# Chunk 0 of six batches: the second expert product by plain matmuls in place of a seven-product block scheme

## The chip, the cores and the metric

The kernel runs on one core of a Trainium2 chip. The metric is the device time of one execution in microseconds. The kernel before was timed in three runs. The profiler also left one execution of it, with the start and end of nearly every instruction on TensorE (PE for matmuls, PEld for the loads of their stationary operand), VectorE (DVE), ScalarE (ACT), GpSimd (POOL) and the queues of the DMAs.

## What is computed

The input is `x` of 8 batches, 2496 rows and 256 columns. Each batch goes through a spectral step and then through one expert of a small mixture of experts.

```python
X = np.fft.rfft(x, axis=1)
Yr = Xr @ w_r - Xi @ w_i + b_r ;  Yi = Xr @ w_i + Xi @ w_r + b_i
Y = shrink(Yr) + 1j * shrink(Yi)        # sign(v) * max(|v| - 0.01, 0)
y = np.fft.irfft(Y, n=2496, axis=1)
e = argmax(softmax(mean(y) @ w_gate))   # one expert per batch
out[b] = gate * (relu(y[b] @ w1[e]) @ w2[e])
```

`w1[e]` is 256 x 1024 and `w2[e]` 1024 x 256. The change lies in the last product, `h @ w2[e]`, whose inner length is 1024.

## The kernel before

**The work of a batch.** The transform of 2496 = 39 x 64 points is done in two steps by matmuls with tables. For batches 2 to 7 (`add_attn`) a forward step over 39 points (line 869) is evicted to `A`, goes through DRAM to `XB`, and is followed by a step over 64 points (L933, evicted to `XT` at L941), the products with the mixed weights (L971), a bias and sum on VectorE (`tt` L985, `z` L995), the shrink (`cl` L1004, `Y` L1010), and the inverse step over 64 points with 64 rows of the array at a time (L599). After another way through DRAM the last inverse step (L1109) is evicted to `ysb` (L1125, L1131). Batches 0 and 1 go through `add_attn_direct` with other shapes.

**The expert's part** (`add_moe`) cuts the 2496 rows of batches 1 to 7 into chunks of 512 rows, c = 0 to 3, and a last one of 448. For each chunk the first product is eight groups of two matmuls of 512 columns (L1445), each evicted with a relu into the tile `hs` (L1458 on ScalarE or L1460 on VectorE). The second product has two forms, and the set `FAST` (L398) says which chunk gets which.

- **Plain form** (L1469 to L1558). A chunk has two tiles of 256 rows. Each tile is 16 matmuls of 256 columns (L1496), four groups of four, into one PSUM bank. One eviction of 128 x 512 then multiplies by the gate (L1513 on ScalarE, L1516 on VectorE), and one DMA stores 256 rows (L1536).
- **Block form** (`add_fast`, L1256). The product is split into 2 x 2 blocks by rows and by inner halves and columns, and done with seven block products in place of eight. VectorE makes four sums of `hs` halves (L1274, L1277, L1281, L1284; 128 x 1024 each). Seven block products of eight matmuls of 128 columns follow (L1307). Four results are taken from PSUM with the gate (L1322 on ScalarE, or L1325 on VectorE), three are added onto them on VectorE (L1331), and two DMAs store 256 rows each (L1358). The block form also needs four sums of `w2` blocks for each batch, `T` (L1249, `add_weight_sums`), which serve all chunks of that batch.

Before the change chunks 0 to 3 of batches 1 to 7 use the block form, 28 chunks. The last chunk of a batch has one plain tile and one turned tile (`add_turned`, L1378, L1393 to L1415); batch 7's last chunk has two plain tiles.

**The order of the work** is not written by hand. Every operation is given to a small planner (`Schedule`) with modelled costs, its dependencies, its buffers and a due time. The planner repeatedly emits the operation that can start first on its engine by its model, and of those that tie the one with the earlier due time. Evictions may go to ScalarE or VectorE, whichever the planner finds free. The order so found is static for each engine; a change of one operation's kind can so reorder others. In units of a period's 44th from a batch's start, the plain groups of chunk 0 are due at 6 to 13, the block products of chunk 0 at 8 to 15.2 with stores at 16, and the first products of chunk 1 at 8 to 15.

**Buffers around it.** `hs` has two buffers. PSUM has four banks "a", two "h" (first product) and two "o" (second product); in batches 1 to 6 a block-form chunk holds both "o" banks from its first products to its last additions, and a plain tile holds one. The sums of `hs` have one buffer, `S`, so the sums of a chunk wait for the last product that reads those of the chunk before. The output tiles `ost` have four buffers.

Of the kernel before, what the change touches and what calls it, by code (L numbers as in the profile page):

```python
# [17 lines left out]
B = 8  # L18
# [232 lines left out]
def kernel(  # L251
# [143 lines left out]
    W_LATE, B_LATE = 46.0, 53.5  # L395
    WARM, COLD, WARM_END = 60, 12, 11.9
    LATE = -0.12
    FAST = {(B - 1, c) for c in range(4)} | {(b, c) for b in range(1, B - 1) for c in (0,1,2,3,)}  # L398
    PERIOD, SPAN, SHIFT = 49.5, 1.4, 0.6

    ps = psum.tile([P, 8, 512], FP32, name="ps")
# [835 lines left out]
    def add_weight_sums(b, w, wk, v):  # L1237
        tk = S.tok("T", 1)

        t_ops = []  # L1240
        for i in (0, 1, 2, 3):
            def ts(_, i=i):
                if i == 0:
                    T_t[b] = spool.tile([P, 4, 4, P], FP16, name="T")
                T = T_t[b]
                w2 = w2s_t[b].rearrange("p (k i) (h c) -> p k h i c", k=2, h=2)
                x, y = ((w2[:, 0, 1], w2[:, 0, 0]), (w2[:, 1, 1], T[:, 0]),
                        (w2[:, 1, 1], w2[:, 0, 1]), (w2[:, 1, 0], T[:, 1]))[i]
                nc.vector.tensor_sub(out=T[:, i], in0=x, in1=y)  # L1249
            t = S.op("DVE", 0.35, ts, v, deps=[w] + t_ops[-1:], lat=0.48,  # L1250
                     allocs=[] if i else [tk])
            wk.rel.append(t)
            t_ops.append(t)
        return t_ops, tk
# [166 lines left out]
    def add_moe(b, y_ops, yk, gate):  # L1421
        w, gb_op, wk = gate
        v0 = b * PERIOD
        if any(x == b for x, _ in FAST):
            t_op = add_weight_sums(b, w, wk, v0 - 0.05 * PERIOD)
            t_first = t_op[0][0]
        for c, (ns, nl, tiles) in enumerate(NCH0 if b == 0 else NCH):
# [36 lines left out]
            if c == 0 and 0 < b < B - 1:  # L1464
                t_first.after = h_ops[0]
            if (b, c) in FAST:
                add_fast(b, c, ns, nl, cell, h_ops, hk, wk, t_op, gb_op, v0)
# [136 lines left out]
```

## Time and profile before

| | |
|---|---|
| three runs | 430.68, 429.89, 430.34 us; median 430.34 |
| the profiled execution | 430.68 us, its span 428.9 us |
| granted TensorE clock | 1.000 over the span |
| busy share of the span | PE 97%, PEld 73%, DVE 80%, ACT 83%, POOL 14% |
| DMA | 77.72 MB, mean 181 GB/s |

The span runs from the first to the last instruction. A PE row is drawn longer than the time that it keeps the array, since the next matmul starts before the one before it has drained: a matmul of 128 columns shows a mean of 219 ns. What a matmul costs a stream of matmuls is read from the chain of work that ended last, which gives runs of equal matmuls from start to start. Idle time of an engine that is not the bottleneck costs nothing.

### The profile page before, as it was taken

How to read it: one execution, taken by the hardware profiler on the slowest of the kernel's cores; microseconds unless marked ns; L12 is line 12 of the kernel's file. 1: busy time of each engine (PE TensorE's matmuls, PEld its weight loads, DVE VectorE, ACT ScalarE, POOL GpSimd, SP SyncE). 2: the span in 40 equal slices, each digit the busy share in tenths (PEclk: the TensorE clock that was granted, in tenths of full speed). 3: DMA queues.
4: the chain of work that ended last, by engine and by line, in shares of the span. 5: the costliest groups of instructions: out<-in, count | busy, mean ns of one | idle time of the engine just before them, and what ended most of it. 6: DMA issues, size and time to landing. Idle time of an engine off the chain costs nothing.

```text
span 428.9 us, 11121 instructions
## 1 busy us (share of the span) xinstructions
PE 415.3 (97%) x4297; PEld 311.9 (73%) x4297; DVE 344.6 (80%) x667; ACT 357.3 (83%) x742; POOL 60.7 (14%) x104
## 2 busy tenths in 40 slices
PE   5888999999999999999999999999999999999996
PEld 2557777887677867778677876778677876777775
DVE  1697875767889899898998889988998989966661
ACT  3788888888978798888978799787978888788884
POOL 5463100001003020033002120031200030001000
PEclk9999999999999999999999999999999999999999
DMA  8899797939786996879985997969976294532222
GB/s 148 228 172 166 129 274 241 252 92 178 205 265 126 226 219 200 265 131 232 198 235 176 217 214 196 287 109 240 210 210 227 76 198 93 166 108 79 66 100 92
DMA packets 70973, 77.72 MB, mean 181 GB/s; under 512 B 7144, under 2 KB 43712, under 8 KB 70920
## 3 DMA queue, kind: packets, MB, share of 16 engines
q1 hardware_dynamic: 57954, 56.88, 45.4%
q0 software_dynamic: 12704, 19.88, 29.2%
q8 instruction: 33, 0.54, 0.5%
q10 hardware_dynamic: 262, 0.25, 0.2%
q14 instruction: 20, 0.16, 0.1%
HBM read 58.20 MB, written 37.49 MB: 223 GB/s over the span
## 4 chain that ended last, share of the span: by engine, by line
PE 87%; DVE 7%; ACT 2%; DMA 2%; issue 1%; POOL 1%; DVEq 0%; POOLq 0%
PE ps L1445 30%; PE ps L1307 21%; PE ps L971 8%; PE ps L1496 7%; PE ps L599 4%; PE ps L1109 4%; PE ps L869 3%; PE ps L775 3%; PE ps L933 3%; PE ps L1378 2%; DMA xin<-in_x_dram 2%; DVE tt L985 1%; DVE z L823 1%; DVE z L995 1%; PE ps L811 1%
## 5 line engine op out<-in xcount | busy, mean ns | idle before, releaser
L1458 ACT ACTIVATE hs<-ps 128x512 f16<-128x512 f32 (+3 forms) x307 | 167.5, 575 | 31.2 <-PE ps L1445 27.0
L1445 PE MATMUL ps<-ysb,w1s 128*128 128x512 f16 (+3 forms) x688 | 179.6, 359 | 0.3 <-ACT hs L1458 0.3
L1445 PEld LDWEIGHTS <-w1s 128*128 128x128 f16 x688 | 68.0, 113 | 22.2 <-issue 2.4
L1307 PEld LDWEIGHTS <-hs 128*128 128x128 f16 x896 | 58.1, 98 | 17.9 <-issue 2.5
L1322 ACT ACTIVATE ost<-ps,gbc 128x256 f32<-128x256 f32 x111 | 53.8, 485 | 9.2 <-PE ps L1307 8.4
L1331 DVE SCALAR_TENSOR_TENSOR ost<-ps,gbc,ost 128x256 f32<-128x256 f32 x84 | 40.4, 480 | 18.9 <-ACT ost L1322 12.7
L1307 PEld LDWEIGHTS <-S 128*128 128x128 f16 x672 | 42.9, 98 | 11.3 <-issue 0.4
L971 PE MATMUL ps<-w,XT 128*128 128x256 f16 x360 | 49.9, 273 | 0.0
L971 PEld LDWEIGHTS <-XT 128*128 128x128 f16 x360 | 34.8, 98 | 12.8 <-DVE XT L952 0.2
L995 DVE TENSOR_TENSOR z<-ps,tt 128x512 f16<-128x512 f32 x60 | 39.3, 685 | 2.5 <-PE ps L971 1.3
L1496 PE MATMUL ps<-w2s,hs 128*128 128x256 f16 x288 | 40.7, 272 | 0.0
L985 DVE TENSOR_TENSOR tt<-ps,bias 128x1024 f16<-128x1024 f32 x30 | 36.6, 1221 | 4.2 <-PE ps L971 3.8
L1307 PE MATMUL ps<-T,hs 128*128 128x128 f16 x448 | 34.2, 219 | 0.0
L1307 PE MATMUL ps<-w2s,hs 128*128 128x128 f16 x448 | 34.2, 219 | 0.0
L1125 ACT CAST ysb<-ps 128x468 f16<-128x468 f32 (+1 forms) x67 | 31.7, 526 | 2.8 <-PE ps L1109 1.9
L879 ACT CAST A<-ps 120x512 f16<-120x512 f32 x57 | 32.9, 622 | 0.8 <-PE ps L869 0.3
L1307 PE MATMUL ps<-T,S 128*128 128x128 f16 x448 | 32.7, 219 | 0.0
L941 ACT CAST XT<-ps 128x512 f16<-128x512 f32 x52 | 30.1, 613 | 0.2 <-PE ps L933 0.2
L1496 PEld LDWEIGHTS <-hs 128*128 128x128 f16 x288 | 26.9, 98 | 3.9
L1460 DVE TENSOR_SCALAR hs<-ps 128x512 f16<-128x512 f32 (+3 forms) x37 | 21.2, 588 | 10.3 <-PE ps L1445 9.9
L609 ACT CAST V<-ps 128x512 f16<-128x512 f32 x42 | 23.7, 601 | 5.5 <-PE ps L599 5.4
L1201 POOL DMA_DIRECT2D w1s<-in_moe_w_dram x8 | 6.0, 754 | 123.9 <-DVE z L995 67.3
(116 smaller groups left out, 631.5 us busy)
## 6 DMA issues: line engine op xcount, KB each, us to landing
out_dram<-ost SPq DMA_DIRECT2D x71, 256.0 KB
scr<-V SPq DMA_DIRECT2D x35, 256.0 KB
xin<-in_x_dram POOLq DMA_DIRECT2D x21, 390.0 KB, 9.0
XB<-fwd SPq DMA_DIRECT2D x30, 256.0 KB
V<-scr SPq DMA_DIRECT2D x14, 504.0 KB
fwd<-A SPq DMA_DIRECT2D x18, 360.0 KB
w1s<-in_moe_w_dram POOLq DMA_DIRECT2D x8, 512.0 KB, 6.3
w2s<-in_moe_w_dram POOLq DMA_DIRECT2D x8, 512.0 KB, 7.9
```

The costliest lines, as they stand in the source:

```text
L879: COPY[eng](out=A_t[b][:, 2 * gp : 2 * gp + 2, :].rearrange("p g c -> p (g c)"), in_=cell["p"][0:120, :])
L941: COPY[eng](out=cell["X"][:, ch, :, 0:2].rearrange("p a r i k -> p a i r k"), in_=hc["p"].rearrange("p (a i r k) -> p a i r k", a=2, i=2, ...
L971: nc.tensor.matmul(pm[:, D * a : D * a + D], cell["X"][:, ch, a, t].rearrange("p i k -> p (i k)"), w4[:, ch, t, :], start=(ch == 0), stop= ...
L985: nc.vector.tensor_add(out=cell["tt"], in0=cell["T", 2].rearrange("p (a c) -> p a c", a=2).unsqueeze(1).to_broadcast([P, 2, 2, D]), in1=bi ...
L995: nc.vector.tensor_add(out=cell["z"][:, r], in0=cell["T", 1 - r].rearrange("p (a c) -> p a c", a=2), in1=cell["tt"][:, r])
L1125: COPY[eng](out=yv[:, :, 12 * gb : 12 * gb + 3 * nf].rearrange("p a (g j) -> p a g j", j=3), in_=pi[:, 0 : 117 * nf].rearrange("p (g a j) ...
L1307: nc.tensor.matmul(fc[dst[0]][0:m, dst[1], t, :], A[a](f, t), bb(f), start=start and t == 0 and f == 0, stop=f == 3, skip_group_check=True)
L1322: nc.scalar.activation(out=ost(t, h), in_=src, func=AFT.Copy, scale=gbc_t[b][0:m])
L1331: nc.vector.scalar_tensor_tensor(out=ost(t, h), in0=fc["F"][0:m, half], scalar=gbc_t[b][0:m], in1=ost(t, h), op0=ALU.mult, op1=ALU.add)
L1445: nc.tensor.matmul(ph[:, 0:nl], w1v[:, ch, fc // 4, :, fc % 4], ysb_t[b][:, ch, ns : ns + nl], start=(ch == 0), stop=(ch == 1))
L1458: nc.scalar.activation(out=o, in_=i, func=AFT.Relu)
L1496: nc.tensor.matmul(oc["p"][:, i, :], cell["hs"][:, ft, ts], w2s_t[b][:, ft, :], start=(ft == 0), stop=(ft == E - 1))
```

## The change

Chunk 0 of batches 1 to 6 leaves the set `FAST`. These six chunks are computed in the plain form; chunks 1 to 3 of those batches and chunks 0 to 3 of batch 7 stay in the block form. Nothing else is edited.

```diff
-    FAST = {(B - 1, c) for c in range(4)} | {(b, c) for b in range(1, B - 1) for c in (0,1,2,3,)}
+    FAST = {(B - 1, c) for c in range(4)} | {(b, c) for b in range(1, B - 1) for c in (1,2,3,)}
```

The set is read in two places: at L1424, where the sums `T` are made for each batch that has any chunk in it (batches 1 to 7 still do), and at L1466, where a chunk takes the one form or the other. A short label that came with the change speaks of an inverse step in half-array matmul pairs and a shrink in one operation over all partitions. The diff touches neither; the inverse step at L599 and the shrink at L1004 and L1010 stay as they are.

## Prediction

> **What bounds the kernel now.** I read the page first: busy shares, then the costliest groups.
>
> ```profile
> span 428.9 us, 11121 instructions
> PE 415.3 (97%) x4297; PEld 311.9 (73%) x4297; DVE 344.6 (80%) x667; ACT 357.3 (83%) x742; POOL 60.7 (14%) x104
> L1322 ACT ACTIVATE ost<-ps,gbc 128x256 f32<-128x256 f32 x111 | 53.8, 485 | 9.2 <-PE ps L1307 8.4
> L1331 DVE SCALAR_TENSOR_TENSOR ost<-ps,gbc,ost 128x256 f32<-128x256 f32 x84 | 40.4, 480 | 18.9 <-ACT ost L1322 12.7
> ```
>
> PE is busy for 97% of the span. A PE row is modelled, though, so the share alone doesn't say that PE is the limit. Next come the windows: four equal stretches of 49.5 us, a batch each, and the two that follow.
>
> ```profile
> 139.50:189.00 49.50, 49.46 (x539) 37.35 (x536) 44.91 (x86) 43.15 (x94) 7.59 (x13) 1.00 0.86 207
> 189.00:238.50 49.50, 49.46 (x539) 37.34 (x537) 44.91 (x86) 43.14 (x94) 7.70 (x13) 1.00 0.87 208
> ...
> 337.50:387.00 49.50, 48.73 (x540) 36.84 (x538) 41.28 (x76) 40.65 (x88) 3.71 (x6) 1.00 0.51 125
> 387.00:428.90 41.90, 38.01 (x405) 28.94 (x401) 21.42 (x41) 31.09 (x67) 2.28 (x4) 1.00 0.25 86
> ```
>
> After the start and length stand PE, PEld, DVE, ACT, POOL, the clock (1.00), the DMA share and GB/s. In a full period PE is without work for 0.04 us, DVE for 4.6, ACT for 6.4. From 90 to 337.5 us the list of waits names no wait of a matmul at all (only of weight loads, 0.4 us at most). In 337.5 to 387 it names two (0.44 us for `tt` L985, 0.29 us for `hs` L1458), and PE is idle for 0.77 us.
>
> The third view is the chain of work that ended last. In a full period every piece of it is PE. These pieces (start, length, what, how many) give the prices:
>
> ```profile
> 170.32 0.87 PE ps L971 x8
> ...
> 175.59 0.54 PE ps L599 x8
> 176.14 1.00 PE ps L1307 x16
> ...
> 179.77 0.89 PE ps L1307 x16
> ...
> 342.80 0.88 PE ps L1496 x8
> ```
>
> Sixteen matmuls of 128 columns take 0.89 us, so 55.6 ns each. Eight of 256 columns take 0.87 (L971) or 0.88 us (L1496), so 109 to 110 ns. Behind a group of L599, which uses half the rows, the next group is some 0.11 us longer (1.00 against 0.89), whichever it is.
>
> Is anything hidden in "busy"? I add up a period at these prices. L1445: 64 x 216.5 ns + 16 x 190 = 16.9 us (pairs of 0.43 and 0.38); L1307: 224 x 55.6 = 12.45; L971: 60 x 109 = 6.54; L599: 40 x 67.5 = 2.70; L1109: 42 x 52 and two short ones = 2.23; L869: 11 x 216 = 2.38; L933: 40 x 56 = 2.24; L1496: 16 x 109 = 1.74; L1378: 16 x 82.5 = 1.32; the gate 0.1. That is 48.6 us, and five L599 groups with 0.11 behind each make it 49.15. The period is 49.5, so 0.35 us is left open. **PE's own work is the bound, and the others' slack is real.** A microsecond taken from DVE is worth nothing here; a microsecond added to PE costs a microsecond.
>
> **The change, part by part** (six chunks, one in each of batches 1 to 6).
>
> PE: each chunk loses seven block products, 56 matmuls of 128 columns: 56 x 55.6 ns = 3.11 us. It gains 32 matmuls of 256 columns: 32 x 109.5 = 3.50 us. That is +0.39 us a chunk, at most +0.41 (0.88 us for eight). A lower price: L1307 holds 25.8% of the chain of a full period, 12.77 us or 3.19 a chunk, because some L599 pauses stand before it; against 3.49 the difference is 0.30. Those pauses don't leave with the form, so I take 0.385. **Six chunks: +2.3 us**, bounds 1.8 and 2.45.
>
> A rule that speaks against this: the Trainium skill, "TensorE: Matmul & The Clock Gate", section "Back-to-back issue gap", says that in a stream of weight loads and matmuls the loads count too, and gives about 81 ns for a matmul of 128 columns and about 131 ns for 512. By it, and with about 98 ns for 256 columns drawn between the two, an estimate from that page, a chunk would go from 4.5 to 3.1 us and the change would win some 8 us. The 0.89 us for sixteen in this trace, each with a load of its own, speaks for 55.6 ns, and the trace decides.
>
> DVE: each chunk loses four sums of 0.683 us (L1274 to L1284) and three additions of 0.480, together 4.17 us. ACT: it loses four takes of 0.485 us (1.94) and gains two evictions of 128x512 at 0.689 us (L1513; 0.751 if VectorE takes one), so -0.56 us. In a period DVE goes from 44.9 to about 40.7 us. Both lie beside PE's 49.5, so I count them at **nothing**. What could be regained is bounded by PE's idle time: 0.04 us a period, 0.15 in 90 to 139.5, 0.77 in 337.5 to 387. In that last stretch the 0.29 and 0.44 us end at 350.87 and 357.35; the first sum of batch 6's chunk 0 (L1274) begins at 357.21. Most of that idle time comes before the sums that go, and the sums `T` (four of 0.42 us, 350.7 to 353.5) stay, as chunk 1 needs them. I take 0, with -0.9 as the end of all idle time regained.
>
> Buffers, waits and queues, all with one answer. A plain tile holds one "o" bank where the block form held both. The sums of chunk 1 no longer wait for chunk 0's use of `S`. `hs` is held until the last plain group, as it was until the last block product. An eviction now waits for sixteen matmuls; behind it on ACT stand relu evictions with 6.4 us of slack a period. Two stores of 256 KB go to SP's queue before and after, due a little earlier. The weight load and its GpSimd DMAs don't move. Cost: nothing, and if that cover fails, PE shows it as a wait.
>
> The order: the planner finds a new one, and no row shows it. Where PE is packed, a different order of the same work costs nothing. Where DVE holds the chain, at 101 to 110 us and 352 to 357 us, an unlucky order could make PE wait for a `tt` (1.22 us) once more, and a lucky one saves the idle time above. I take 0, which is nearest to the windows' idle times, with +1.2 and -0.9 as ends.
>
> **Sum.** The profiled execution took 430.68 us (span 428.9 and 1.78 around it), the slowest of the three; +2.3 gives 433.0. Against the median 430.34 that is 432.6, which I forecast. The own range of this case: 430.34 + 1.8 - 0.9 = 431.2 to 430.34 + 2.45 + 1.2 = 434.0.
>
> **Rivals.**
>
> *Faster, as VectorE is relieved.* Mechanism: the 0.9 us by which a period (49.5) exceeds my sum of PE's work (48.6) is not the pause behind L599 but PE waiting for evictions inside rows drawn as busy; with 4.2 us less on DVE these waits go. All of it: six chunks x (0.385 - 0.9) = -3.1, less 0.77 in the stretch after 337.5 us = -3.9, so 426.5; with half of the 0.9 it is 429.2. It decides from 0.385 us regained a batch. For it: DVE is above 90% busy in the periods, and the matmul ends are modelled. Against it: no DVE or ACT piece in the chain of a period, no wait of PE in the list, and the 0.11 us stands behind L599 at regular places.
>
> *Slower by more, through the order.* In both stretches where DVE holds the chain the new list puts the second product ahead of the eviction that PE needs next, and PE waits for a `tt` and two `z` (1.22 + 1.28 us) in each: 2 x 2.5 + 2.3 = +7.3, so up to 437.6; half of that is 435.3. For it: the work is placed statically by modelled costs. Against it: evictions have more slack than before.
>
> *No difference.* The diff doesn't do what its label says (inverse and shrink stay), and if the plain groups fill pauses that the block products can't, the extra 0.385 us is absorbed: 430.3. Against it: there is no PE idle time to fill in a period.
>
> **How the numbers follow.** Forecast 0.70, faster through VectorE 0.10, slower through the order 0.14, no difference 0.06. A measurement of this kernel can tell about 0.2%, or 0.86 us, from no change: the bounds are 429.5 and 431.2. Faster takes 0.08 of the first rival. Same takes its other 0.02, the 0.06 of no difference, and 0.02 of the forecast's low end: 0.10. Slower is 0.82. The range goes from 430.2, which takes in no difference, to 434.6, which takes in the forecast and nearly half of the slower rival: about 0.82 in all.
>
> **What would show it.** PE should lose 336 rows of L1307 and gain 192 of L1496, whose runs of eight in the chain still take 0.87 to 0.88 us. DVE's busy time should fall by about 25 us (6 x 4.17) to some 320 and ACT's by about 3. The windows of a period should be 49.9 us long with PE idle for less than 0.1, and the last instruction of batch 1's stretch should be late by 0.4, batch 6's by 2.3. If the span grows by more, the list of waits should name PE waiting for DVE or ACT around 100 to 110 or 345 to 365 us. The prediction is wrong in its core if a period becomes shorter than 49.5 us, for then PE's busy rows held waits.

## The result and the profile after

The changed kernel takes 435.35 us (median of four runs, 434.92 to 435.77) against 430.51 for the kernel before. The ratio is 1.0114, with a 95% interval of 1.0097 to 1.0132. The forecast was 432.6 in a range that ended at 434.6: the sign was right, and the loss was about twice as large. The profiled executions have spans of 428.9 and 434.0 us, so 5.1 us are to be found.

From the page of the kernel after, the busy shares and the two groups that show the change:

```profile
span 434.0 us, 10803 instructions
PE 418.2 (96%) x4153; PEld 312.3 (72%) x4153; DVE 330.6 (76%) x635; ACT 353.2 (81%) x720; POOL 60.6 (14%) x104
L1496 PE MATMUL ps<-w2s,hs 128*128 128x256 f16 x480 | 69.3, 273 | 0.0
L1331 DVE SCALAR_TENSOR_TENSOR ost<-ps,gbc,ost 128x256 f32<-128x256 f32 x66 | 31.6, 479 | 14.1 <-ACT ost L1322 10.3
```

L1496 has 192 more matmuls, L1331 18 fewer additions, and VectorE is busy for 14 us less in all (not the 25 of the sum, since the planner gave it more evictions: `V` L609 24 times in place of 18, `A` L879 14 in place of 9). The windows of the kernel after:

```profile
139.50:189.00 49.50, 48.79 (x498) 36.34 (x496) 41.65 (x75) 41.09 (x86) 7.59 (x13) 1.00 0.83 204
189.00:238.50 49.50, 48.79 (x493) 36.39 (x493) 41.61 (x78) 41.07 (x87) 6.11 (x11) 1.00 0.84 202
```

PE, first after the length, now idles for 0.71 us in each of these stretches, where it idled for 0.04. VectorE is less busy than before, and yet PE waits. The list of waits of PE names one line, in the full periods (us in total, times, the longest):

```profile
PE ps L599 <- DVE tt L985: 2.7, 4, 0.7
```

Where do the 5.1 us lie? A mark that each batch has once is the load of `w2` (L1206). It fetches the weights of the batch that comes next, so the stretch from one mark to the following one holds the chunks of one batch. Two of its starts in the kernel after:

```profile
150.84 0.73 POOL L1206 DMA_DIRECT2D w2s<-in_moe_w_dram  x1 [5.30 <-PE ps L1109]
201.68 0.71 POOL L1206 DMA_DIRECT2D w2s<-in_moe_w_dram  x1 [5.28 <-PE ps L1109]
```

From mark to mark a period is 50.84 us; it was 49.51. The table has all such stretches. The last column is for a kernel told below, the block form with a repaired planner:

| from mark to mark, us | before | after | difference | block form, repaired |
|---|---|---|---|---|
| batch 1 | 49.36 | 49.42 | +0.06 | 48.71 |
| batches 2 to 5, each | 49.50 | 50.85 | +1.34 | 49.50 |
| batch 6 to the end | 80.18 | 79.78 | -0.40 | 79.47 |

The four periods together make +5.37, and with 0.07 ahead of batch 1 and -0.34 in the other two rows the sum is 5.1. So the whole loss lies in the four packed periods, 1.34 us in each, of which the prediction's price of the plain form explains 0.385.

**What PE waits for.** The timeline of the kernel after, in the first full period (start, length, engine and line, what; some of PE's rows, and VectorE's `tt`):

```profile
156.04 0.60 PE L1496 MATMUL ps<-w2s,hs 128*128 128x256 f16 x4
...
156.48 0.38 PE L869 MATMUL ps<-xin,wa 117*120 117x512 f16 x1
...
157.57 0.60 PE L971 MATMUL ps<-w,XT 128*128 128x256 f16 x4
...
158.00 0.60 PE L869 MATMUL ps<-xin,wa 117*120 117x512 f16 x2
158.20 1.22 DVE L985 TENSOR_TENSOR tt<-ps,bias 128x1024 f16<-128x1024 f32 x1
...
158.53 0.28 PE L599 MATMUL ps<-Y,ti 64*128 64x256 f16 x1
159.48 0.59 PE L599 MATMUL ps<-Y,ti 64*128 64x256 f16 x7 [0.67 <-DVE tt L985]
```

And the same place in the kernel before:

```profile
155.93 0.81 PE L869 MATMUL ps<-xin,wa 117*120 117x512 f16 x3
...
157.44 0.60 PE L971 MATMUL ps<-w,XT 128*128 128x256 f16 x4
...
157.88 0.61 PE L1307 MATMUL ps<-w2s,hs 128*128 128x128 f16 x8
158.08 1.23 DVE L985 TENSOR_TENSOR tt<-ps,bias 128x1024 f16<-128x1024 f32 x1
158.42 0.61 PE L599 MATMUL ps<-Y,ti 64*128 64x256 f16 x8
```

In both, `tt` runs while PE comes to the third L599 group of a batch. Before, the group's eight matmuls run through. After, one runs, and the other seven wait until `tt` has ended. An L599 group writes two PSUM banks in turn, the first matmul to the one and the second to the other. The four "a" banks are handed out in a ring. Before, the ring ran L869 (three banks), L971, then L599's two: these were banks of L869 groups already evicted. After, the plain form's first group, due at 6 where the block product was due at 8, has taken the place of two L869 groups. They now stand behind L971. The ring runs L869, L971, L869, L869, then L599's two, and with four banks the second of these is the bank of L971, which `tt` is reading.

Why did the planner place an operation that can't run? A token is the planner's claim on one buffer. An operation can take several, and L599 takes two of one bank each (lines of the kernel, shortened, the comments added here):

```python
for k in o.allocs:
    if k.tag in self.rings:
        prev = self.rings[k.tag].owners(k)      # starts at self.at for every k
...
m = S.mm([256] * 4, mmv, vt, deps=[oy, t2_in[0]], allocs=vk + [Vk])   # vk: two tokens "a"
```

The ring moves on only when the tokens are taken. In the check of readiness both tokens look at the same bank, and the holder of the second is not seen. The dependence itself is kept when the kernel runs, so PE waits there, with everything behind it.

### The profile page after: what moved, and what is told of

It is laid out like the page before. It is cut to its first block, busy times and chain, and to the rows that moved or that the text cites. A ratio compares the mean times of both kernels' runs of the same rounds, so it can differ in the third digit from the quotient of the medians.

```text
span 434.0 us, 10803 instructions
## 1 busy us (share of the span) xinstructions
PE 418.2 (96%) x4153; PEld 312.3 (72%) x4153; DVE 330.6 (76%) x635; ACT 353.2 (81%) x720; POOL 60.6 (14%) x104
## 4 chain that ended last, share of the span: by engine, by line
PE 89%; DVE 5%; DMA 2%; ACT 1%; issue 1%; POOL 1%; SPq 0%; DVEq 0%; POOLq 0%
PE ps L1445 30%; PE ps L1307 16%; PE ps L1496 12%; PE ps L971 8%; PE ps L775 4%; PE ps L599 4%; PE ps L1109 4%; PE ps L869 3%; PE ps L933 3%; PE ps L1378 2%; DVE tt L985 2%; DMA xin<-in_x_dram 1%; PE ps L808 1%; PE ps L811 1%; DMA ysb<-in_w_i_dram 1%
## 5 line engine op out<-in xcount | busy, mean ns | idle before, releaser
L1496 PE MATMUL ps<-w2s,hs 128*128 128x256 f16 x480 | 69.3, 273 | 0.0
L1307 PEld LDWEIGHTS <-hs 128*128 128x128 f16 x704 | 46.1, 98 | 14.4 <-issue 1.1
L1496 PEld LDWEIGHTS <-hs 128*128 128x128 f16 x480 | 44.8, 98 | 14.9 <-issue 2.3
L971 PE MATMUL ps<-w,XT 128*128 128x256 f16 x360 | 49.7, 272 | 0.0
L1322 ACT ACTIVATE ost<-ps,gbc 128x256 f32<-128x256 f32 x88 | 42.3, 481 | 7.9 <-PE ps L1307 7.5
L971 PEld LDWEIGHTS <-XT 128*128 128x128 f16 x360 | 34.6, 98 | 10.9 <-DVE XT L952 1.5
L1331 DVE SCALAR_TENSOR_TENSOR ost<-ps,gbc,ost 128x256 f32<-128x256 f32 x66 | 31.6, 479 | 14.1 <-ACT ost L1322 10.3
L995 DVE TENSOR_TENSOR z<-ps,tt 128x512 f16<-128x512 f32 x60 | 39.2, 684 | 3.6 <-PE ps L971 2.9
L1307 PEld LDWEIGHTS <-S 128*128 128x128 f16 x528 | 33.8, 98 | 10.5 <-issue 1.3
L879 ACT CAST A<-ps 120x512 f16<-120x512 f32 x52 | 30.3, 600 | 1.9 <-PE ps L869 1.5
L1307 PE MATMUL ps<-w2s,hs 128*128 128x128 f16 x352 | 26.9, 219 | 0.0
L1307 PE MATMUL ps<-T,hs 128*128 128x128 f16 x352 | 26.8, 219 | 0.0
L609 ACT CAST V<-ps 128x512 f16<-128x512 f32 x36 | 20.5, 587 | 7.6 <-PE ps L599 7.5
L1307 PE MATMUL ps<-T,S 128*128 128x128 f16 x352 | 26.0, 219 | 0.0
L609 DVE CAST V<-ps 128x512 f16<-128x512 f32 x24 | 16.6, 692 | 10.7 <-PE ps L599 10.7
L1460 DVE TENSOR_SCALAR hs<-ps 128x512 f16<-128x512 f32 (+3 forms) x31 | 17.4, 571 | 9.1 <-PE ps L1445 8.9
```

The lines of the kernel that those rows point to most:

```text
L609: COPY[eng](out=hc["V"].rearrange("p (a i) c -> p i a c", i=2)[:, i], in_=hc[i].rearrange("p (a c) -> p a c", a=2))
L879: COPY[eng](out=A_t[b][:, 2 * gp : 2 * gp + 2, :].rearrange("p g c -> p (g c)"), in_=cell["p"][0:120, :])
L971: nc.tensor.matmul(pm[:, D * a : D * a + D], cell["X"][:, ch, a, t].rearrange("p i k -> p (i k)"), w4[:, ch, t, :], start=(ch == 0), stop= ...
L995: nc.vector.tensor_add(out=cell["z"][:, r], in0=cell["T", 1 - r].rearrange("p (a c) -> p a c", a=2), in1=cell["tt"][:, r])
L1307: nc.tensor.matmul(fc[dst[0]][0:m, dst[1], t, :], A[a](f, t), bb(f), start=start and t == 0 and f == 0, stop=f == 3, skip_group_check=True)
L1322: nc.scalar.activation(out=ost(t, h), in_=src, func=AFT.Copy, scale=gbc_t[b][0:m])
```

## The experiments

**Theory.** In each of four periods PE waits some 0.95 us (1.34 less 0.385) for the second bank of the third L599 group. The first rival is the form's price: the plain form itself costs 1.3 us. The second is order in general: an earlier second product upsets the evictions, whatever the banks.

**The wait without the plain form.** The kernel before, no chunk in plain form, with only the due times of four chunks' block products moved:

```diff
-        vt = lambda x: v0 + PERIOD * (c * 8 + 8 + x) / 44
+        vt = lambda x: v0 + PERIOD * (c * 8 + 8 + x - (1.5 if c == 0 and 1 < b < B - 2 else 0)) / 44
```

> The kernel before, all in block form, with chunk 0's block products of batches 2 to 5 due 1.5 units earlier; no work is added. Bank theory: TensorE's third group of L599 in each of four batches waits for its second PSUM bank, which the sum tt (L985) of the next block is still reading; about 0.95 us each, so 430.5 + 3.8 = 434.3, and four waits of L599 for tt of about 0.7 us in the list besides the one of 0.44 us that was there. Rival, the form's price (the plain form itself costs 1.3 us a chunk in a full period): 430.5, since no chunk is in plain form. Rival, order in general (an earlier second product upsets the evictions, whatever the banks): 431 to 435 with the waits spread over other lines.

Measured: 434.53 us against 430.56 for the kernel before on the same chip, ratio 1.0105 (1.0090 to 1.0121). Its waits of PE:

```profile
PE ps L599 <- DVE tt L985: 3.1, 5, 0.7
```

Its timeline at the place shown above:

```profile
157.11 0.60 PE L971 MATMUL ps<-w,XT 128*128 128x256 f16 x4
157.55 0.60 PE L869 MATMUL ps<-xin,wa 117*120 117x512 f16 x2
157.75 1.22 DVE L985 TENSOR_TENSOR tt<-ps,bias 128x1024 f16<-128x1024 f32 x1
158.08 0.28 PE L599 MATMUL ps<-Y,ti 64*128 64x256 f16 x1
159.03 0.59 PE L599 MATMUL ps<-Y,ti 64*128 64x256 f16 x7 [0.67 <-DVE tt L985]
```

The same order of groups, the same split of L599 and the same 0.67 us, without a single plain group added. The fifth wait in the list is the one of 0.44 us that the kernel before has. The period is 50.48 us, so the wait costs 0.97. The form's price as the cause falls.

**The plain form without the wait, by the planner.** The changed kernel, with the check of readiness made to look at each token's own bank:

```diff
-    def owners(self, k):
-        p = self.first(k)
+    def owners(self, k, ahead=0):
+        p = (self.first(k) + ahead) % len(self.owner)
...
+        ahead = {}
         for k in o.allocs:
             if k.tag in self.rings:
-                prev = self.rings[k.tag].owners(k)
+                prev = self.rings[k.tag].owners(k, ahead.get(k.tag, 0))
+                ahead[k.tag] = ahead.get(k.tag, 0) + k.wide
```

> The changed kernel, with the planner made to look at the release of both banks when an operation takes two. The six chunks stay in plain form. Bank theory: the four waits of L599 for tt go, 435.35 - 3.8 = 431.5, a period of about 49.9 us in place of 50.85. Rival, the form's price: 435.4. Rival, order in general: 433 to 435, other waits in place of these.

Measured: 431.29 us, ratio to the kernel before 1.0019 (1.0009 to 1.0029). No wait of that line is left. One of its windows (the edit moves later lines by two, so L599 is L601 there):

```profile
189.00:238.50 49.50, 49.46 (x507) 36.92 (x505) 41.63 (x77) 42.30 (x90) 7.75 (x13) 1.00 0.86 206
```

PE is full again in this window, with six plain chunks and VectorE at 41.6 us. The period is 49.95 us.

**The plain form without the wait, by due times.** The changed kernel with the planner as it was and the plain groups of chunk 0 due 3 units later:

```diff
-                    v = v0 + PERIOD * (x + 6 * nl / 512 + 4 * sp + q) / 44
+                    v = v0 + PERIOD * (x + 6 * nl / 512 + 4 * sp + q + (3 if c == 0 and 0 < b < B - 1 else 0)) / 44
```

> The changed kernel with the plain groups of chunk 0 due 3 units later (9 to 16 in place of 6 to 13), the planner untouched, so that the forward step's evictions keep their place ahead of the third L599 group. Bank theory: no wait of L599 for tt in a full period, 431.5, by the same sum as with the planner's edit. Rival, the form's price: 435.4. Rival, order in general: anything from 431 to 435.

Measured: 431.40 us, ratio 1.0023 (1.0013 to 1.0033), a period of 49.83 us, no wait of L599's matmuls for `tt`. In both versions the third L599 group now comes behind the end of `tt` and runs whole. In the version by the planner:

```profile
157.67 1.22 DVE L987 TENSOR_TENSOR tt<-ps,bias 128x1024 f16<-128x1024 f32 x1
...
159.30 0.61 PE L601 MATMUL ps<-Y,ti 64*128 64x256 f16 x8
```

In the one by due times:

```profile
159.33 1.23 DVE L985 TENSOR_TENSOR tt<-ps,bias 128x1024 f16<-128x1024 f32 x1
...
160.96 0.61 PE L599 MATMUL ps<-Y,ti 64*128 64x256 f16 x8
```

Two quite different edits that keep the group off a bank still being read give the same time.

**The kernel before with the repaired planner.** The same edit, applied to the block form:

> The kernel before with the same edit of the planner. Bank theory: only the one wait of 0.44 us near 357 us can go, 430.1. Both rivals: 430.5.

Measured: 429.54 us, ratio 0.9973 (0.9958 to 0.9989): the fastest version of this study. The gain is larger than the 0.44 us that I had expected. The last column of the table above shows where it lies: 0.65 us come back in batch 1 and 0.71 behind batch 6. Behind batch 6 it is the wait that the list named in the kernel before:

```profile
356.63 0.28 PE L599 MATMUL ps<-Y,ti 64*128 64x256 f16 x1
...
357.35 0.59 PE L599 MATMUL ps<-Y,ti 64*128 64x256 f16 x7 [0.44 <-DVE tt L985]
```

The seven matmuls start 0.72 us after the first, which keeps the array for about 0.07 (eight take 0.54 us in the chain). So this wait costs about 0.65 us, not 0.44. In batch 1 the list of waits of the kernel before names nothing; there the wait is inside a row drawn as busy:

```profile
109.48 0.97 PE L599 MATMUL ps<-Y,ti 64*128 64x256 f16 x8
```

Eight such matmuls are otherwise drawn with 0.61 us. The chain of work shows the same place as a wait:

```profile
109.20 0.61 DVE z L995
...
109.86 0.59 PE ps L599 x7
```

By the same count of the ring (three L971 groups, two of L869, then L599's two) the second bank is one that `z` (L995) is still reading. The wait costs some 0.31 us (109.86 less 109.48 less 0.07). With the repaired planner the chain through this place is PE alone.

**Holding the bank for a shorter time.** The changed kernel with its order as it was, but `tt` made in two instructions, of which only the first reads PSUM (`first["bd"]` is the difference of the biases, made once; the second half of `tt` is rounded once more):

```diff
+                if "bd" not in first:
+                    first["bd"] = cpool.tile([P, D], FP32, name="biasd")
+                    nc.vector.tensor_sub(out=first["bd"], in0=bias[:, 1],
+                                         in1=bias[:, 0])
                 nc.vector.tensor_add(
-                    out=cell["tt"], in0=cell["T", 2].rearrange(
-                        "p (a c) -> p a c", a=2).unsqueeze(1).to_broadcast(
-                        [P, 2, 2, D]),
-                    in1=bias.unsqueeze(2).to_broadcast([P, 2, 2, D]))
+                    out=cell["tt"][:, 0], in0=cell["T", 2].rearrange(
+                        "p (a c) -> p a c", a=2),
+                    in1=bias[:, 0].unsqueeze(1).to_broadcast([P, 2, D]))
+                nc.vector.tensor_add(
+                    out=cell["tt"][:, 1], in0=cell["tt"][:, 0],
+                    in1=first["bd"].unsqueeze(1).to_broadcast([P, 2, D]))
```

> The changed kernel with the same plan, but the sum tt is made in two instructions: the first reads PSUM and makes half of tt (128x512, some 0.69 us by the rows of L995), the second makes the other half from the first half and the difference of the biases, without PSUM. The bank is held 0.53 us less (0.69 against 1.22), VectorE works 0.15 us more for each tt. Bank theory: each of the four waits gets shorter by about 0.53 us of its 0.95, so 435.35 - 2.1 = 433.2. Rival, order in general: the order of the work is the same and VectorE has more to do, so 435.4 or more.

Measured: 434.09 us, ratio 1.0060 (1.0032 to 1.0088) to the kernel before, which took 430.94 on this chip. The 433.2 expected were counted from 430.51, a ratio of 1.0062, so the ratio came as expected, within a wide interval. In the timeline of the full period:

```profile
158.49 0.68 DVE L989 TENSOR_TENSOR tt<-ps,bias 128x512 f16<-128x512 f32 x1
...
158.78 0.28 PE L599 MATMUL ps<-Y,ti 64*128 64x256 f16 x1
159.20 0.69 DVE L993 TENSOR_TENSOR tt<-tt,biasd 128x512 f16<-128x512 f16 x1
159.22 0.59 PE L599 MATMUL ps<-Y,ti 64*128 64x256 f16 x7 [0.17 <-DVE tt L989]
```

The wait is 0.17 us in place of 0.67, and the seven matmuls start as the first instruction ends, while the second half of `tt` still runs. The period falls by 0.46 us, to 50.39, near the 0.53 expected. So it is the reading of the bank that PE waits for, not `tt` as such. Batch 1 took 49.83 us, 0.41 more than in the changed kernel. There the third L599 group waits for `z` behind two `tt`, as shown above, and each `tt` now takes 0.68 and 0.69 us in two instructions where it took 1.22; the seven matmuls start 8.90 us after the mark in place of 8.51.

**Batches 1 and 6 alone.** The kernel before with two plain chunks:

```diff
-    FAST = {(B - 1, c) for c in range(4)} | {(b, c) for b in range(1, B - 1) for c in (0,1,2,3,)}
+    FAST = {(B - 1, c) for c in range(4)} | {(b, c) for b in range(1, B - 1) for c in (0,1,2,3,) if c or b not in (1, 6)}
```

> The kernel before with chunk 0 in plain form in batches 1 and 6 alone, the planner untouched. By the distances between the loads of w2 in the two profiles, batch 1 cost +0.06 us and the stretch from batch 6 to the end -0.4 us under the change. If these belong to the two chunks themselves: 430.2, no loss. Rival: each plain chunk costs its 0.385 us wherever it stands: 431.3.

Measured: 430.39 us against 430.94, ratio 0.9976 (0.9960 to 0.9992). These two chunks bring no loss, though each adds the same matmuls: the distances between the marks show it, 49.41 us for batch 1 and 79.80 behind batch 6. Under the repaired planner the same places have the usual price (49.10 against 48.71 us, and 79.82 against 79.47, with and without plain chunks). So the block form's old order held waits there that the plain form's order is without, and the traces name them. Behind batch 6 the third L599 group is no longer split, as the chain of the changed kernel shows:

```profile
362.39 0.54 PE ps L599 x8
```

That takes away the 0.65 us of the wait shown above, and with the price of 0.39 the sum is -0.26; measured are -0.40 in the changed kernel. In batch 1 the wait for `z` stays: the seven matmuls of that group start 8.51 us after the mark in the kernel before, in the changed one and in this one. What is gone is a second wait, of a block product for ScalarE's take, from the chain of the kernel before:

```profile
115.59 0.39 ACT ost L1322
...
116.02 0.61 PE ps L1307 x8
```

The four matmuls of L933 ahead of it start at 115.58 and take 0.22 us, so PE stands still for about 0.22 us before this product. The chain of the changed kernel has no such piece. That is most of the 0.33 us by which batch 1 stayed below the price; the rest is open.

**The price alone.** The repaired planner with plain chunks in batches 2 to 5:

```diff
-    FAST = {(B - 1, c) for c in range(4)} | {(b, c) for b in range(1, B - 1) for c in (0,1,2,3,)}
+    FAST = {(B - 1, c) for c in range(4)} | {(b, c) for b in range(1, B - 1) for c in (0,1,2,3,) if c or b in (1, 6)}
```

> The planner with the edit that looks at both banks, chunk 0 in plain form in batches 2 to 5 alone, to be set against the block form with the same edit (429.54). With no wait for a bank only the form's price is left: 4 x 0.45 (a period of 49.95 against 49.50 in the profiles with this edit) = +1.8, so 431.3; by the prices of the prediction 4 x 0.385 = +1.5, so 431.1. If the plain form cost nothing when no bank is in the way: 429.5.

Measured: 431.04 us, ratio 0.9993 (0.9977 to 1.0009) to the kernel before, which took 430.94 on this chip. The median is 1.50 us above the 429.54 of the block form with the same planner, but that was timed on another chip, and by the two ratios (0.9993 and 0.9973) the distance is only some 0.9 us, with intervals as wide as that. The marks tell it more closely: the four periods together are 1.76 us longer in the profile (49.94 to 49.95 us each against 49.50), while batch 1 (48.70 against 48.71) and the stretch behind batch 6 (79.45 against 79.47) are the same. That is 0.44 us a chunk; four times the forecast 0.385 is 1.54.

## Why the prediction was wrong

**What bounds the kernel** was right. Where no bank is in the way, PE is full with either form (49.46 us of a window of 49.50), and less work on VectorE brought nothing.

**PE's price** was right to within 0.06 us a chunk: 0.385 was forecast, with +0.41 as the most. Free of waits a period grows by 0.33 (later due times) to 0.45 us (repaired planner). L1496 still takes 0.44 us for four matmuls in the chain.

**The order** is the step that failed: "Where PE is packed, a different order of the same work costs nothing. [...] I take 0". In a packed period the new order cost 0.90 to 1.02 us (50.85 against 49.95 and 49.83 in the two versions without the wait), in four periods about 3.8 us. That was outside my end of +1.2, which I had placed on one wait in a stretch where VectorE holds the chain. An absence of waits in the old order said nothing about the new one. The list of waits was to name PE around 100 to 110 or 345 to 365 us; it named the full periods. The reason was in sight: the wait of 0.44 us for `tt` at 357.35 in the kernel before is the same split of an L599 group in one and seven, and it goes with the repaired planner. I took it for a shortage of VectorE in a thin stretch. By the prediction's own price the whole is 2.3 us for six chunks, plus 3.8 for the four waits, less 1.1 in the two other stretches: 5.0 of the 5.1 us between the profiles. The sign of the forecast came from the price, which holds; most of the loss came from the wait.

**Buffers**: "A plain tile holds one "o" bank where the block form held both" looked at the banks of the changed work alone. What moved was the forward step's claim on the "a" banks.

**The rival "slower through the order"** was right in kind, PE waiting for `tt` by a static order, and wrong in place and price: it set 2.5 us in each of two thin stretches. These two gave 0.33 and 0.8 us less than the price of their chunks asked for (+0.06 and -0.40 in place of +0.39 each). Half of that rival's waits, 430.34 + 2.3 + 2.5, would also be 435.1 us, not the 435.3 given; that the measured 435.35 lies beside it is chance. **The rival "faster, as VectorE is relieved"** fell: from mark to mark VectorE had 2 us less to do in the changed kernel and 3 us less with the repaired planner (42.9 and 42.05 us in place of 44.9), and the period grew in both. But its remark that busy rows can hide waits held for batch 1, where 0.31 us of waiting stood in a row drawn as busy.

## What to carry to other kernels

When operations are placed by a planner, an edit that only exchanges one form of work for another also moves its neighbours in every ring of buffers. Count, around the edit, which buffer the next multi-buffer operation takes and who still reads it. A wait that appears once in a profile of a repeating schedule deserves its cause, since a shift by one place can bring it into every period. A planner's check of readiness has to see all the buffers that it will take. Where the list of waits is silent, the chain of work can still show a wait: a piece of another engine that ends just before a group starts.

## What the runs showed of the hardware

A wait of PE in the middle of a group is shown shorter than it costs: the list gave 0.67 us where a period grew by 0.90 to 1.02, since the matmul ahead of the wait is drawn with 0.28 us and keeps the array for about 0.07 (0.54 us for eight in the chain). 0.67 + 0.28 - 0.07 is 0.88 us. A wait can also be missing from the list and show as a group drawn too long (0.97 against 0.61 us).
